# Attention and feed-forward in one kernel: inputs cast to bf16 by the GpSimd DMA queue, feed-forward started one batch earlier

## The chip, the cores and the metric

One core of one Trainium2 chip. The metric is device time of one execution in microseconds (us), the median of three or four runs of a kernel (of seven for the kernel before in the experiments). The span is the time from the first to the last instruction in the profile. Every ratio is taken against runs of the kernel before on the same chip in the same rounds.

## The reference

Eight batches of attention (8 heads, 576 queries, 576 keys plus 16 beacon keys that every query sees, head size 64), then a gated feed-forward over all 4608 tokens:

```python
k_all = np.concatenate([beacon_k, k], axis=2); v_all = np.concatenate([beacon_v, v], axis=2)
scores = scale * np.matmul(q, k_all.transpose(0, 1, 3, 2))      # causal on the last 576 keys
a = softmax(scores); attn = np.matmul(a, v_all)                 # (8, 8, 576, 64)
x = attn.transpose(0, 2, 1, 3).reshape(4608, 512)
g = x @ w_gate                                                  # 512 -> 1536
out = (g * sigmoid(g) * (x @ w_val)) @ w_out                    # float32
```

The inputs are float32; the kernel computes in bf16.

## The kernel before

Work is cut into units that the program weaves together by hand. For a pair of heads: first and second half of the scores (`s_ps`), exponentials on ScalarE, causal selects on POOL (the GpSimd engine), and two PV products (the exponentials times v, one product a head: `pv_ps`, 15 matmuls of 65 columns each). For the feed-forward: a "gv unit" (8 matmuls of 512 columns into `gv_ps`, then tanh on ScalarE and the products `u` and `hT` on VectorE) and single output matmuls into `o_ps`. A batch has four steps, one for each pair of heads. In the views, PE is TensorE, PEld its weight loads, DVE VectorE, ACT ScalarE, SPq the queue of SyncE; `xT` is the attention result x, transposed.

The inputs of batches 2 to 7 travel so: SyncE loads float32 rows into staging tiles; VectorE casts q and k, POOL casts v; SyncE issues DMA transposes that put q and k in the form that the scores need (`qT`, `kT`).

```python
def load_batch(b):                        # 31 DMAs on SyncE
    first = load_kv(nc.sync, "k32", k, beacon_k, b, 0, H)
    load_q(nc.sync, b, 0, H)
    load_kv(nc.sync, "v32", v, beacon_v, b, 0, H)
    return first

def prep_pieces(b):
    pieces = []
    for c in range(NKT):
        pieces.append(
            lambda c=c: (cast_chunk(kb, "k32", c, nc.vector), dma_transpose(kT, kb, 80, b, c)))
        pieces.append(
            lambda c=c: (cast_chunk(qb, "q32", c, nc.vector), dma_transpose(qT, qb, 64, b, c),
                         cast_chunk(vb[b % 2], "v32", c, nc.gpsimd)))
    return pieces
# ... batches 0 and 1: attention alone, q and k transposed by TensorE; then 24 gv units
#     and 36 output matmuls without attention, while batch 2 is loaded; then:
for b in range(2, B):
    for m in range(NPAIR):
        if m == 2 and b + 1 < B:
            pieces = prep_pieces(b + 1)
        G()                               # a gv unit, if one is queued
        scores1(b, m)
        if prev: pv(*prev, 0)
        F(6)                              # six output matmuls, if queued
        # ... two pieces, if m >= 2
        scores2(b, m)
        # ... at m == 1: queue the gv units and output matmuls of earlier batches
        G()
        # ... one piece; second pv; F(6)
        if prev and m == 0:
            x_transpose(b - 1)            # five DMA transposes on SyncE
        if m == 0 and b + 1 < B:
            load_batch(b + 1)
        G()
        # ... two pieces
        prev = (b, m)
```

The softmax here doesn't subtract the row's maximum and nothing guards it: scores larger than these inputs give would overflow.

## Time and profile before

| | before |
|---|---|
| median of 3 runs | 509.77 us (507.91 to 511.09) |
| span of the profiled run | 503.9 us |
| mean granted TensorE clock, as recorded | 0.929 |
| start of batch 3 (its first scores start at 169.9, wait, and go on at 173.4) | 172 us |

The table of stretches, the chain and the waits stand in the prediction below. The queue of SyncE in the timeline, in a batch that loads (start, us held, queue, line, operation, output and input, count):

```profile
227.61 6.42 SPq L257 DMA_TRANSPOSE xT<-x  x5
...
236.01 4.27 SPq L118 DMA_DIRECT2D k<-in_k_dram  x8
...
247.64 4.57 SPq L118 DMA_DIRECT2D v<-in_v_dram  x8
...
253.40 1.25 SPq L166 DMA_TRANSPOSE kT<-kb  x1
```

In this trace the queue issues in program order. After the five x-transposes it issues loads until past 252 us, and only then the first transpose for the next batch. The page's line for the DMA queue that carries these loads (packets, MB, share of 16 engines' span):

```profile
q1 hardware_dynamic: 162400, 47.94, 43.6%
```

### The profile page before, as it was taken

Reading aid. Unit: us, or ns where it says so; the run is one execution under the profiler, and the core shown is the slowest. Engines: PE = TensorE matmul, PEld = TensorE weight load, DVE = VectorE, ACT = ScalarE, POOL = GpSimd, SP = SyncE. Lnnn points to the kernel's source line nnn. Section 1 sums busy time; section 2 is a strip of 40 time slices with the busy share of each in tenths; the row PEclk is TensorE's granted clock in tenths of the full one; section 3 lists DMA queues with packets and bytes.
Section 4 is the critical chain, followed back from the end, with each engine's and each line's share of the span. In section 5 each row is a group of like instructions: output and inputs, shape, how many; then the busy total and the mean of one; then the engine's idle time right before and its main releaser. Section 6 shows DMA issues by size and latency. Waiting matters only on the chain.

```text
span 503.9 us, 7659 instructions
## 1 busy us (share of the span) xinstructions
PE 403.4 (80%) x2718; PEld 192.3 (38%) x2760; DVE 256.1 (51%) x506; ACT 170.7 (34%) x237; POOL 121.5 (24%) x393
## 2 busy tenths in 40 slices
PE   1688879995564259768886997699769998999996
PEld 0355544442232124334332443244324443444442
DVE  2455437885026014735563637454745656456662
ACT  1555413330351134434433443344325441122220
POOL 6554640010135030511141105120503110000000
PEclk9999999999697579879987998899879999999999
DMA  8763896484299329814981397239924102100102
GB/s 166 171 151 89 127 140 111 104 184 104 54 208 181 79 74 204 141 33 97 206 148 44 72 197 186 71 70 194 186 45 69 43 21 69 53 32 21 43 21 104
DMA packets 171078, 54.35 MB, mean 108 GB/s; under 512 B 160592, under 2 KB 166256, under 8 KB 171040
## 3 DMA queue, kind: packets, MB, share of 16 engines
q1 hardware_dynamic: 162400, 47.94, 43.6%
q0 software_dynamic: 6112, 5.33, 6.8%
q10 hardware_dynamic: 2528, 0.61, 0.7%
q8 instruction: 21, 0.34, 0.3%
q14 instruction: 17, 0.14, 0.1%
HBM read 38.27 MB, written 9.44 MB: 95 GB/s over the span
## 4 chain that ended last, share of the span: by engine, by line
PE 52%; SPq 20%; DVE 12%; DMA 8%; issue 3%; ACT 2%; another core or an unknown queue 1%; ACTq 0%; POOL 0%; DVEq 0%; POOLq 0%
PE gv_ps L269 25%; PE o_ps L298 15%; PE pv_ps L228 6%; SPq L257 5%; SPq L118 5%; SPq L106 4%; PE s_ps L191 4%; DVE u L280 3%; DVE hT L283 3%; DMA qT<-qb 3%; DMA v<-in_v_dram 3%; SPq L166 2%; DVE x L237 2%; PE t_ps L158 2%; ACT th L278 1%
## 5 line engine op out<-in xcount | busy, mean ns | idle before, releaser
L200 ACT ACTIVATE p<-s_ps 128x720 bf16<-128x720 f32 (+1 forms) x128 | 105.0, 874 | 126.2 <-PE s_ps L191 118.8
L202 POOL TENSOR_SCALAR_AFFINE_SELECT p<-p 128x112 bf16<-128x112 bf16 (+2 forms) x320 | 82.4, 291 | 201.0 <-ACT p L200 197.4
L278 ACT ACTIVATE th<-gv_ps 128x512 f32<-128x512 f32 x108 | 64.5, 597 | 183.5 <-PE gv_ps L269 160.9
L280 DVE SCALAR_TENSOR_TENSOR u<-th,gv_ps 128x512 f32<-128x512 f32 x108 | 74.1, 686 | 102.0 <-ACT th L278 101.7
L269 PE MATMUL gv_ps<-xT,wg 128*128 128x512 bf16 x419 | 114.9, 393 | 8.2 <-DMA xT<-x 6.6
L298 PE MATMUL o_ps<-wo,hT 128*128 128x512 bf16 x412 | 110.7, 406 | 3.4 <-DVE o_sb L307 2.1
L269 PE MATMUL gv_ps<-xT,wv 128*128 128x512 bf16 x423 | 111.5, 385 | 0.2
L191 PE MATMUL s_ps<-qT,kT 64*128 64x336 bf16 (+5 forms) x384 | 51.0, 343 | 52.6 <-DMA qT<-qb 35.3
L283 DVE SCALAR_TENSOR_TENSOR hT<-gv_ps,u 128x512 bf16<-128x512 f32 x108 | 74.7, 691 | 3.7
L269 PEld LDWEIGHTS <-wg 128*128 128x128 bf16 x432 | 41.6, 100 | 58.2 <-issue 13.6
L269 PEld LDWEIGHTS <-wv 128*128 128x128 bf16 x432 | 43.0, 99 | 53.5 <-issue 4.4
L298 PEld LDWEIGHTS <-hT 128*128 128x128 bf16 x432 | 41.6, 103 | 49.2 <-issue 11.9
L228 PE MATMUL pv_ps<-vb,p 128*128 128x65 bf16 x960 | 49.0, 211 | 10.3 <-DVE x L237 8.1
L228 PEld LDWEIGHTS <-p 128*128 128x128 bf16 x960 | 42.7, 109 | 27.5 <-issue 17.7
L191 PEld LDWEIGHTS <-kT 64*128 64x128 bf16 x384 | 16.3, 105 | 85.5 <-issue 57.9
L307 DVE COPY o_sb<-o_ps 128x512 f32<-128x512 f32 x36 | 24.8, 688 | 37.9 <-PE o_ps L298 36.0
L140 POOL CAST vb<-v 128x512 bf16<-128x512 f32 (+1 forms) x30 | 18.7, 638 | 87.0 <-DMA v<-in_v_dram 87.0
L236 DVE RECIPROCAL rec<-pv_ps 128x5 f32<-128x5 f32 x64 | 12.1, 190 | 42.3 <-PE pv_ps L228 42.3
L237 DVE TENSOR_TENSOR x<-pv_ps,rec 128x320 bf16<-128x320 f32 x64 | 31.5, 492 | 2.2
L140 DVE CAST qb<-q 128x512 bf16<-128x512 f32 (+1 forms) x30 | 13.4, 448 | 29.3 <-DMA v<-in_beacon_v_dram 19.6
L140 DVE CAST kb<-k 128x512 bf16<-128x512 f32 (+1 forms) x30 | 14.1, 470 | 0.0
L158 PE MATMUL t_ps<-ident,kb 128*128 128x128 bf16 (+1 forms) x40 | 5.8, 299 | 8.7 <-DVE kb L135 7.5
(33 smaller groups left out, 69.8 us busy)
## 6 DMA issues: line engine op xcount, KB each, us to landing
out_dram<-o_sb SPq DMA_DIRECT2D x36, 256.0 KB, 2.2
q<-in_q_dram SPq DMA_DIRECT2D x70, 128.0 KB, 3.4
k<-in_k_dram SPq DMA_DIRECT2D x64, 96.0 KB, 2.8
v<-in_v_dram SPq DMA_DIRECT2D x56, 96.0 KB, 3.2
wg<-in_moe_w_gate_dram POOLq DMA_DIRECT2D x4, 384.0 KB, 6.2
wv<-in_moe_w_val_dram POOLq DMA_DIRECT2D x4, 384.0 KB, 7.8
wo<-in_moe_w_out_dram POOLq DMA_DIRECT2D x2, 768.0 KB, 14.0
k<-in_k_dram SPq DMA_DIRECT2D x6, 224.0 KB, 3.3
```

What stands on the lines that cost most here:

```text
L118: eng.dma_start(d[:, 1:4, h, :], src[b, h, 112:496, :].rearrange("(c p) d -> p c d", p=P))
L140: engine.tensor_copy(dst[0:n, c, :, 0:D], stage[name][0:n, c, :, :])
L191: nc.tensor.matmul(s[hh][:, col : col + n], lhsT=kT[b % 2][r, m, P * t : P * t + P], rhs=qT[b % 2][r, m, q0 : q0 + n], start=True, stop=True,)
L200: nc.scalar.activation(p[:, 0:used], s[hh][:, 0:used], ACT.Exp, scale=0.125)
L202: nc.gpsimd.affine_select(out=p[:, col : col + n], in_=p[:, col : col + n], compare_op=ALU.is_ge, fill=0.0, base=base, pattern=[[1, n]], c ...
L228: nc.tensor.matmul(o_ps[:, c, 0 : D + 1], lhsT=pt[2 * (m % 2) + hh][w][:, col : col + P], rhs=vb[b % 2][:, t, h, 0 : D + 1], start=(t == 0 ...
L237: nc.vector.tensor_tensor(out=xs[b][:, :, D * h : D * h + D], in0=o_ps[:, :, 0:D], in1=rec[:].to_broadcast([P, NKT, D]), op=ALU.mult,)
L269: nc.tensor.matmul(ps[:, TOK * half : TOK * half + TOK], lhsT=w[:, kk, P * f : P * f + P], rhs=xT[:, kk, r : r + TOK], start=(kk == 0), st ...
L278: tanh = nc.scalar.activation(th[:], ps[:, 0:TOK], ACT.Tanh, scale=0.5)
L280: nc.vector.scalar_tensor_tensor(out=u[:], in0=th[:], scalar=1.0, in1=ps[:, 0:TOK], op0=ALU.add, op1=ALU.mult)
L283: nc.vector.scalar_tensor_tensor(out=hTs[j][:, f, :], in0=ps[:, TOK:1024], scalar=0.5, in1=u[:], op0=ALU.mult, op1=ALU.mult)
L298: nc.tensor.matmul(st["o"][:], lhsT=hTs[j][:, f, P * i : P * i + P], rhs=wo[:, f, :], start=(f == 0), stop=(f == NF - 1),)
```

## The change

Its intent: take the loads off SyncE and the casts off VectorE and POOL by letting the GpSimd DMA queue cast while it loads, straight into double-buffered bf16 tiles; start the feed-forward while batch 1 still computes its attention, so that the stretch of feed-forward alone disappears. The core of the diff:

```diff
+NPE = 3
     ... (three buffers of o_sb instead of two; in the tail 18 output matmuls ahead instead of 12)
-    stage = {n: static.tile([P, NKT, H, D], FP32, name=n) for n in ("q32", "k32", "v32")}
-    qb = static.tile([P, NKT, H, D], BF16, name="qb")
-    kb = static.tile([P, NKT, H, D], BF16, name="kb")
+    q32 = hT_pool.tile([P, QK], FP32, name="q32", tag="hT")      # batch 0 only
+    q16 = static.tile([P, QK], BF16, name="q16")                 # runs of 1 KB, batches 1 and 2
+    qb = [static.tile([P, QK], BF16, name=f"qb{i}") for i in range(2)]
     ... (k32, k16, kb likewise)
+    def load_runs(b, h0, h1):                                    # 5 DMAs, all on nc.gpsimd
+        load_main(nc.gpsimd, k16, k, b, h0, h1)
+        load_rest(nc.gpsimd, k16, k, beacon_k, b, h0, h1)
+        load_main(nc.gpsimd, q16, q, b, h0, h1)
+        load_rest(nc.gpsimd, q16, q, None, b, h0, h1)
+    def load_tiles(b):                                           # 11 DMAs on nc.gpsimd
+        load_key_tiles(tiles(kb[b % 2]), k, beacon_k, b, 0, H)
+        for c in range(NKT):
+            nc.gpsimd.dma_start(tiles(qb[b % 2])[0:n, c, :, :], q[b, :, P * c : P * c + n, :]...)
     ... (transpose_pair: two VectorE copies from runs to tiles, five TensorE transposes,
          two or three VectorE copies out of PSUM)
     make_identity(nc, ident)
-    load_kv(nc.gpsimd, "v32", v, beacon_v, 0, 4, 8)
+    load_v(0, 0, 4)
+    load_v(0, 4, 8)
+    load_w(0)
     for i in range(2):
-        nc.gpsimd.memset(vb[i][64:P, 4, :, 0:D], 0.0)
+        nc.vector.memset(vb[i][64:P, 4, :, 0:D], 0.0)
     ... (batch 0 alone; then, from batch 1 on:)
+    for s in range(NPAIR, len(steps)):
+        G(); scores1(b, m); pv(*prev, 0); F(6); scores2(b, m)
+        if nxt[0] < NPE:
+            prep_k(*nxt, att, "att")
     ... (m == 1 and b > 1: queue gv units and output matmuls)
+        G(); pv(*prev, 1); F(6)
     ... (m == 0: x_transpose(b - 1))
+        G()
+        if nxt[0] < NPE:
+            prep_q(*nxt, att, "att")
     ... (ten DMA transposes of the next batch from m == 1 on, four a step)
+        if b == 1 and m < 2:
+            load_runs(2, 4 * m, 4 * m + 4)
     ... (b == 1: load_v(2), load_wo)
+        if m == 3 and NPE <= b + 2 < B:
+            load_tiles(b + 2)
+        if m == 1 and NPE <= b + 1 < B:
+            load_v(b + 1, 0, H)
```

## The prediction

> **What bounds the kernel now.** I read the page first, then the chain that ended last, a table of stretches, the waits, and the timeline around the waits. The chain's summary:
>
> ```profile
> PE 52%; SPq 20%; DVE 12%; DMA 8%; issue 3%; ACT 2%; another core or an unknown queue 1%; ACTq 0%; POOL 0%; DVEq 0%; POOLq 0%
> ```
>
> Only half of the end time is TensorE work; a fifth is the SyncE queue issuing DMAs. The stretches (cut at the first scores, the start and end of the first feed-forward, and the starts of batches 2 to 7) show where. Columns: length, busy us of the engines, granted clock, DMA share, GB/s.
>
> ```profile
> 0.00:12.10 12.10, 1.70 (x10) 0.92 (x11) 3.01 (x16) 1.28 (x1) 8.23 (x19) 1.00 0.90 170
> 12.10:69.60 57.50, 43.37 (x446) 27.71 (x447) 28.96 (x82) 26.25 (x32) 34.20 (x104) 1.00 0.67 128
> 69.60:121.00 51.40, 51.05 (x223) 22.65 (x226) 37.45 (x60) 14.33 (x24) 2.89 (x5) 1.00 0.69 134
> 121.00:132.00 11.00, 0.82 (x4) 0.23 (x4) 1.27 (x3) 0.00 (x0) 0.00 (x0) 0.68 0.50 121
> 132.00:172.00 40.00, 21.23 (x182) 9.21 (x185) 11.78 (x26) 13.16 (x16) 13.59 (x45) 0.80 0.74 146
> 172.00:217.60 45.60, 32.35 (x248) 15.26 (x252) 21.25 (x45) 18.36 (x25) 13.42 (x45) 0.84 0.64 125
> 217.60:270.00 52.40, 40.94 (x291) 18.88 (x295) 26.17 (x52) 20.25 (x28) 13.09 (x45) 0.89 0.57 115
> ...
> 372.50:415.00 42.50, 41.76 (x304) 19.48 (x309) 22.17 (x42) 19.73 (x27) 10.03 (x40) 0.94 0.17 39
> 415.00:503.90 88.90, 82.48 (x402) 37.80 (x407) 49.23 (x75) 16.72 (x28) 0.00 (x0) 1.00 0.14 49
> ```
>
> Two stretches are full of TensorE work (the feed-forward at 69.6 and the tail). Batch 7, which loads nothing, takes 42.5 us with TensorE full; batch 4, with loads, 52.4. What the loading batches wait for:
>
> ```profile
> PE s_ps L191 <- DMA qT<-qb: 35.3, 11, 8.1
> ...
> 128.76 0.61 PE L191 MATMUL s_ps<-qT,kT 64*128 64x512 bf16 x2 [7.88 <-DMA qT<-qb]
> ...
> 249.25 0.43 DVE L140 CAST qb<-q 128x512 bf16<-128x512 f32 x1 [5.60 <-DMA q<-in_q_dram]
> ...
> 253.68 0.57 PE L191 MATMUL s_ps<-qT,kT 64*128 64x512 bf16 x3 [2.25 <-DVE hT L283]
> ```
>
> A batch's first scores wait for the last DMA transpose; that waits its turn on SyncE behind 31 loads and 5 other transposes; and VectorE, in order, stands still at a cast whose load has not landed, holding up the hT behind it.
>
> Sizes at full clock, from the chain in order of time (start, us, work):
>
> ```profile
> 36.23 0.95 PE pv_ps L228 x15
> ...
> 42.23 0.77 PE t_ps L158 x5
> ...
> 45.41 0.93 PE s_ps L191 x4
> ...
> 480.99 0.86 PE o_ps L298 x4
> 481.86 1.73 PE gv_ps L269 x8
> ```
>
> The second half of the scores takes 0.76 us there too. So full-clock TensorE work before is 108 gv units x 1.73 = 186.8, 432 output matmuls x 0.215 = 92.9, 32 head pairs x (0.93 + 0.76 + 2 x 0.95) = 115.2, 16 q/k pair transposes x 0.77 = 12.3, 8 x-transposes at about 0.7 = 5.6: 413 us. The span is 503.9, so about 91 us are losses: 10 at the start, 12 in batches 0 and 1, 12 plus a cold clock before batch 2, some 15 in batch 2 and in batch 3, 5 to 9 in each of batches 4 to 6, the rest small.
>
> **What the Trainium skill says.** "TensorE: Matmul & The Clock Gate", Part 1, says an idle window of about 3.4 us halves the matmul clock. The trace agrees: 0.68 in the 11 us with TensorE nearly idle, 1.00 in the full stretches; so lost waits also repay in clock. "DMA: Bandwidth & Descriptors", "SWDGE vs HWDGE vs iDMA", says a cast during DMA goes only through GpSimd, whose cores compute the descriptors. The trace has this for the weights: POOL is held 0.765 us for a wg load of 512 rows, 0.751 for a v load of 384, 0.875 for wo of 768. "Perfetto Trace Analysis", "DMA Instruction — SWDGE (GPSIMD)", says such a recorded interval ends with the descriptors written, not with the data; agreed, as the v loads held POOL 0.75 us and landed 5.0 us after issue.
>
> **The change, part by part.**
>
> Removed: VectorE casts of k and q for batches 2 to 7 (60 x about 0.46 = 27 us of VectorE, little of it on the path in itself), the 46 casts of v on POOL (26 us), and SyncE's 31 load issues per batch (about 0.5 us each). SyncE keeps 10 + 5 transposes at 1.25 us and 4 stores, some 21 us of a batch. In the compiled order the 10 transposes of the next batch come four, four and two at the ends of steps 1, 2 and 3; the last two are free to issue about 6 us into step 3 (after that step's store) and land near 11 us, before the scores that need them at about 13. So the wait for qT should go in batches 3 to 7.
>
> Added on POOL: 11 issues for k and q and 6 for v per batch, up to 1024 rows each. From 0.751 at 384 and 0.875 at 768 I estimate 0.95 us for 1024: 10 us in one block at the end of step 3, and 5.5 at the end of step 1. Selects are about 3 us a step. The block runs from about 8 us of step 3 to 18 or 20; the next step's selects then end at about 23, while PV needs them at about 25. Just hidden.
>
> Added on TensorE: batch 2's q and k transposes (8 x 0.77), minus 4 x 0.7 as batch 1's x goes by DMA: work rises to about 416 us.
>
> Start, which gets worse: in the compiled order VectorE's second instruction, a memset of vb's lower rows, stands after the v loads in the program and waits for two of them, the last being the twelfth DMA on POOL. Twelve issues from 1.6 us at about 0.74 end at 10.4; landing about 13.5 to 14.5. Memsets 0.8, then copy, transpose, PSUM copy for k and again for q: about 4.3 us (the strided PSUM copies I put at 0.65 us, between the 0.466 of the plain bf16 one and the 0.688 of o_sb, plus small ones). First scores at about 19 against 12.1: +7. (The order also zeroes 16 loaded rows of v, which costs no time.)
>
> Batch 0: steps of about 7 to 8 us (6.77 before), the PSUM copies being longer. After steps 0 and 1 POOL issues 11 loads, 8 us, before the next selects, so PV slips by about 1 and then 3 us. Batch 1's first scores at about 50.
>
> Batch 1 with feed-forward: a step has 3 gv units (5.2), scores and PV (3.6) and two transposes (1.54), 10.3 us of work. But the q transposes stand after the third gv unit, and their VectorE copy behind that unit's hT: TensorE waits for tanh 0.60 + u 0.69 + hT 0.69 + copies 0.7 + handovers, about 2.8 us, and about 0.9 more for k and buffers. Step about 14.1; the first, with little gv, about 14.6; batch 1 ends at about 107. Batch 2: 12 + 17 (five x-transposes on SyncE, 6.4 + 2.4 us, delay its first gv unit of chunk 1) + 16 + 11.4; batch 3 starts near 163, with 20 gv units and 30 output matmuls done. Before started it at 172 to 174, with 24 and 84 done. The missing 4 x 1.73 + 54 x 0.215 = 18.5 us put the new kernel about 8 us *behind* at this point.
>
> Batches 3 to end: remaining work 88 x 1.73 + 402 x 0.215 + 5 x 14.3 = 310 us. Losses: 1.5 us in each of five batches (first gv unit waiting for x-transposes that now share the DMA engines with loads), 5 us in the tail, as now. So 163 + 310 + 7.5 + 5 = 486. The 2.8 us stalls plus a 0.77 us transpose come close to the idle window; I add 4 us for cold clock: 490.
>
> From 172 on the kernel before loses 504 - 172 minus its remaining 292 us, about 40; the new one about 12. The gain of 28 there is eaten by half in the first three batches. Timed, 490 x 509.77 / 503.9 = 495.7; I say 494, a little less as my stalls were all taken in full.
>
> **Rivals.**
> 1. *POOL becomes the bound.* If a 1024-row cast DMA holds POOL 2 us rather than 0.95, the block is 22 us, selects come about 9 us late in each of five batches, and the time is about 535. For it: everything is now on one in-order queue, and in the compiled order each POOL DMA also waits for the one eight before it. Against: the flat 0.67 to 0.875 us over 64 to 768 rows.
> 2. *Everything pipelines.* If the copies of batches 1 and 2 run ahead and the stalls shrink, only work is left: 416 + 19 start + 6 batch 0 + 12 = 453 span, about 460. For it: TensorE was at 7.9 of 8 us in batch 7. Against: VectorE is in order, and the copy stands behind hT.
> 3. *The transfers collide.* Loads of 9344 rows of 256 B run when x-transposes do. At 20 ns a packet (0.80 x 16 engines x 8 us for 1.29 MB in the first 8 us) they take 12 us of all engines. If transposes doubled, 3 to 5 us a batch would be lost: about 512.
>
> **Range and chances.** The two halves pull against each other and each is uncertain by some 8 us, more on the slow side: 480 to 511. Faster than 499.6 is likelier than not.
>
> **What would show it.** Right: first scores near 19 us; PE t_ps waits on VectorE of 2 to 3 us in batches 1 and 2; batch 3 at about 163; no qT wait over 2 us after it; batches 4 to 6 at 46 to 48 us; POOL blocks of 10 us. Wrong: POOL issues well over 1 us, PV waiting on selects after batch 2, or batch 3 before 150.

## The result, and the profile after

| | before | after |
|---|---|---|
| median of 4 runs | 508.84 us (506.98 to 511.09) | 455.89 us (454.23 to 457.41) |
| span of the profiled run | 503.9 us | 455.6 us |
| recorded clock | 0.929 | 0.978 |
| start of batch 3 (after: its first gv unit; first scores at 160.7) | 172 us | 158.9 us |
| batches 3 to 7 | 243.0 us | 205.1 us |
| after batch 7 | 88.9 us | 91.6 us |

The ratio is 0.8957, 95% interval 0.8904 to 0.901. Here and below, a ratio is the mean time of one kernel's runs over that of the other's runs of the same rounds, so not quite the ratio of the quoted medians. The changed kernel is 10.4% faster, and its time lies 24 us under the low end of my range.

The summary of the chain that ended last, after:

```profile
PE 62%; DVE 14%; POOL 6%; ACT 5%; another core or an unknown queue 5%; DMA 3%; issue 2%; SPq 2%; POOLq 0%; DVEq 0%
```

SyncE's queue fell from 20% of the end time to 2%; TensorE rose from 52% to 62%. The table of stretches of the kernel after, with the same columns as in the prediction (length, busy us of PE, PEld, DVE, ACT, POOL, clock, DMA share, GB/s); the rows are batch 0's loads, the first step of batch 2, batch 3, and the tail (the clock of 1.00 in the first row stands for no record, see the part on the error):

```profile
0.00:22.90 22.90, 1.45 (x10) 0.92 (x11) 3.76 (x24) 1.28 (x1) 10.57 (x20) 1.00 1.02 165
...
107.90:122.90 15.00, 8.45 (x93) 4.86 (x92) 8.18 (x24) 7.74 (x10) 6.14 (x23) 0.83 0.69 71
...
158.90:199.80 40.90, 39.72 (x305) 18.41 (x309) 23.83 (x44) 20.33 (x28) 22.72 (x57) 1.00 1.03 114
...
364.00:455.60 91.60, 85.23 (x414) 39.07 (x420) 50.52 (x77) 17.32 (x29) 0.00 (x0) 1.00 0.14 47
```

From batch 3 on TensorE is full: 39.7 of 40.9 us, at full clock, while the DMA share is at 1.03 and POOL is busy 22.7 us; none of the two holds it up. Before, the batches that load took 45.6 to 52.4 us. What is lost now is lost early: 22.9 us until the first scores, and steps of batches 1 and 2 that are not full. Their waits (engine, tile, line, releaser, then total us, count, longest):

```profile
DVE vb L373 <- DMA vb<-in_v_dram: 16.4, 1, 16.4
...
PE t_ps L186 <- DVE qb L178: 19.3, 11, 2.5
```

The same in the timeline, where a bracket gives the idle time ahead of an instruction and what ended it; the last two lines are a full step of batch 3:

```profile
17.53 0.27 DVE L373 MEMSET vb<- 64x256 uint32 x1 [16.41 <-DMA vb<-in_v_dram]
...
22.92 1.00 PE L221 MATMUL s_ps<-qT,kT 64*128 64x512 bf16 x4 [0.78 <-DVE qT L189]
...
90.75 0.77 PE L186 MATMUL t_ps<-ident,qb 128*128 128x128 bf16 x5 [2.46 <-DVE qb L178]
...
176.60 0.61 PE L258 MATMUL pv_ps<-vb,p 128*128 128x65 bf16 x15
177.05 1.46 PE L328 MATMUL o_ps<-wo,hT 128*128 128x512 bf16 x5
```

Read starts, not durations, where matmuls are pipelined: the 15 PV matmuls start at 176.60 and the next work at 177.05, so they occupy TensorE for 0.45 us. I had counted 0.95. That line is the key to the error.

The SyncE queue after, in a batch that loads:

```profile
218.66 1.22 SPq L205 DMA_TRANSPOSE kT<-kb  x1
...
238.67 1.21 SPq L205 DMA_TRANSPOSE qT<-qb  x1
```

The transposes now spread over 218 to 240 us, and batch 5's scores come only at 240.9: no wait for qT is left there.

Where the gain arises can be counted. At its start of batch 3 the kernel after is some 13.1 us earlier (172 - 158.9; the two cuts are not the same instruction, see the tables), but has 4 gv units and 54 output matmuls fewer behind it, worth 18.5 us: it is 5 us *behind*, much as predicted. From there to the end it needs 296.7 us against 331.9, with those 18.5 us more to do: it gains 54 us where I had predicted 28.

The kernel after has two faults of data order, which the comparison with the reference lets pass. The memset shown above comes after the v loads and zeroes 16 loaded rows of batch 0's v. And the second half of batch 2's q and k is loaded over heads 6 and 7 of batch 1 before these have been copied out. No run tests why they stay unseen. Put into the numpy reference afterwards, the first changes 16 of the 4608 output rows, by 18% there and 0.2% of the whole (root mean square); the second changes the 576 rows of batch 1, by 1% there: the scores are so small that the softmax is almost uniform. Both are mended in some experiments below, to see whether they cost or save time.

### The profile page after: what moved, and what is told of

Its sections match the earlier page's. It is cut to its first block, busy times and chain, and to the rows that moved or that the text cites. A ratio compares the mean times of both kernels' runs of the same rounds, so it can differ in the third digit from the quotient of the medians.

```text
span 455.6 us, 7472 instructions
## 1 busy us (share of the span) xinstructions
PE 388.6 (85%) x2736; PEld 184.3 (40%) x2780; DVE 245.5 (54%) x506; ACT 170.8 (37%) x237; POOL 193.7 (43%) x477
## 3 DMA queue, kind: packets, MB, share of 16 engines
q0 software_dynamic: 99056, 17.95, 52.2%
## 4 chain that ended last, share of the span: by engine, by line
PE 62%; DVE 14%; POOL 6%; ACT 5%; another core or an unknown queue 5%; DMA 3%; issue 2%; SPq 2%; POOLq 0%; DVEq 0%
PE gv_ps L299 32%; PE o_ps L328 18%; DVE u L310 6%; DVE hT L313 5%; PE pv_ps L258 5%; PE s_ps L221 5%; ACT th L308 5%; POOL vb L146 2%; PE t_ps L186 2%; DMA vb<-in_v_dram 2%; SPq L287 2%; POOL p L232 1%; DMA xT<-x 1%; DVE x L267 1%
## 5 line engine op out<-in xcount | busy, mean ns | idle before, releaser
L232 POOL TENSOR_SCALAR_AFFINE_SELECT p<-p 128x112 bf16<-128x112 bf16 (+2 forms) x320 | 80.3, 297 | 155.8 <-ACT p L230 155.0
L328 PE MATMUL o_ps<-wo,hT 128*128 128x512 bf16 x414 | 103.2, 381 | 3.1 <-DVE o_sb L337 2.1
L328 PEld LDWEIGHTS <-hT 128*128 128x128 bf16 x432 | 39.3, 98 | 42.6 <-issue 3.1
L221 PE MATMUL s_ps<-qT,kT 64*128 64x336 bf16 (+5 forms) x384 | 47.5, 315 | 7.3 <-DVE qT L189 2.4
L258 PEld LDWEIGHTS <-p 128*128 128x128 bf16 x960 | 39.1, 103 | 24.6 <-issue 13.0
L258 PE MATMUL pv_ps<-vb,p 128*128 128x65 bf16 x960 | 45.2, 202 | 4.0 <-POOL p L232 2.4
L146 POOL DMA_DIRECT2D vb<-in_v_dram x44 | 34.4, 809 | 0.1
L186 PE MATMUL t_ps<-ident,qb 128*128 128x128 bf16 (+1 forms) x60 | 8.3, 267 | 19.4 <-DVE qb L178 19.3
L157 POOL DMA_DIRECT2D qb<-in_q_dram x25 | 21.1, 885 | 0.0
L146 POOL DMA_DIRECT2D kb<-in_k_dram x20 | 17.0, 868 | 0.2 <-issue 0.2
```

What stands on the lines that cost most here:

```text
L146: eng.dma_start(dst[0:n, c, h0:h1, 0:D], src[b, h0:h1, r : r + n, :].rearrange("h j d -> j h d"))
L221: nc.tensor.matmul(s[hh][:, col : col + n], lhsT=kT[b % 2][r, m, P * t : P * t + P], rhs=qT[b % 2][r, m, q0 : q0 + n], start=True, stop=True,)
L232: nc.gpsimd.affine_select(out=p[:, col : col + n], in_=p[:, col : col + n], compare_op=ALU.is_ge, fill=0.0, base=base, pattern=[[1, n]], c ...
L258: nc.tensor.matmul(o_ps[:, c, 0 : D + 1], lhsT=pt[2 * (m % 2) + hh][w][:, col : col + P], rhs=vb[b % 2][:, t, h, 0 : D + 1], start=(t == 0 ...
L328: nc.tensor.matmul(st["o"][:], lhsT=hTs[j][:, f, P * i : P * i + P], rhs=wo[:, f, :], start=(f == 0), stop=(f == NF - 1),)
```

## The experiments

Two questions. First: the kernel before had 54 us to win after batch 3 rather than 28; whose were they? Theory S: of SyncE's in-order queue, whose 31 load issues hold back the transposes. Rival V: of VectorE's casts, which stand in order ahead of `hT` and of PSUM copies. Second: did the sizes in my sum fail because of the clock? All kernels here gave results that the comparison accepted.

| run | median us | before | ratio (95%) |
|---|---|---|---|
| m1_memset_first | 445.32 | 506.7 | 0.8777 (0.8735 to 0.8819) |
| m2_q_early | 451.5 | 506.7 | 0.8902 (0.8861 to 0.8943) |
| m3_k16_late | 456.06 | 506.7 | 0.8997 (0.894 to 0.9053) |
| m4_before_swloads | 449.06 | 506.7 | 0.8847 (0.8792 to 0.8903) |
| c1_sp_issues | 502.78 | 508.58 | 0.9893 (0.9826 to 0.996) |
| c3_sp_and_casts | 506.44 | 508.58 | 0.9977 (0.9899 to 1.0054) |
| e1_warm_start | 447.44 | 508.58 | 0.8808 (0.8744 to 0.8871) |
| n2_tiles_from_2 | 434.68 | 508.58 | 0.8572 (0.8501 to 0.8642) |
| n3_free_bank | 425.92 | 508.25 | 0.8368 (0.8316 to 0.8419) |
| n4_spread | 413.93 | 508.25 | 0.8136 (0.8106 to 0.8166) |

### m4_before_swloads: the load part alone, on the kernel before

```diff
 # kernel before, with qb2/kb2: two bf16 tiles each
-            tanh = G()          # and load_batch(2) at f == 5, held back behind it
+            G()                 # load_tiles(2), load_v(2), load_tiles(3) ahead of this loop
-        lambda: (cast_chunk(kb, "k32", c, nc.vector), dma_transpose(kT, kb, ...))
+        lambda: dma_transpose(kT, kb2[b % 2], ...)       # q likewise; no casts
-            if m == 0 and b + 1 < B: load_batch(b + 1)
+            # four pieces at the end of each step from m == 1 on
+            if m == 3 and b + 2 < B: load_tiles(b + 2)   # on nc.gpsimd
+            if m == 1 and b + 1 < B: load_v(b + 1)
```

> The kernel before with only the load part: k, q and v of batches 2 to 7 cast by GpSimd DMA into double bf16 tiles, DMA transposes from step 1 on; batches 0 and 1, and the feed-forward block behind them, as before. Theory A (the gain is the loads: no SyncE backlog, no VectorE casts waiting in order): batches 4 to 7 take 41 us each, none waits for qT over 1 us, batch 2 starts near 122 us, and the time is 425 to 445, so below the changed kernel. Rival B (the gain is the feed-forward woven in from batch 1 on): 475 or more.

Measured: 449.06 us, 57.6 under the kernel before and some 7 *under* the whole change. (By the ratios, 0.8847 against 0.8957, it is 5 to 6 us; the intervals just miss each other.) So the load part carries all of the gain, and the schedule of the first batches, as given, loses some of it again. The edit also issues the transposes one step earlier; it does not tell that apart from the loads' leaving SyncE. The run lies 4 us over my range. What was missing stands in its timeline, at the start of batch 3:

```profile
145.51 0.61 PE L204 MATMUL s_ps<-qT,kT 64*128 64x512 bf16 x2 [5.92 <-DMA qT<-qb]
...
165.96 1.86 PE L282 MATMUL gv_ps<-xT,wg 128*128 128x512 bf16 x4 [6.78 <-DMA xT<-x]
```

Batch 2 is short there, as no feed-forward is woven into it, so batch 3's transposes are issued too late for it.

### c1_sp_issues: SyncE's issues put back into the kernel after, without the data

```diff
+    scr = static.tile([P, 31 * D], FP32, name="scr")
         elif m == 0:
             x_transpose(b - 1)
+            if 2 <= b and b + 1 < B:
+                for i in range(31):      # 16 rows of 256 B each, never used
+                    nc.sync.dma_start(scr[0:16, D*i : D*i+D], k[b+1, 0, 16*i : 16*i+16, :])
```

> The changed kernel with 31 tiny loads a batch (4 KB each, result unused) back on the SyncE queue at the point where the kernel before issues its loads, batches 2 to 6. They cost SyncE about 0.45 us each and the DMA engines almost nothing. Theory S (the loss of the kernel before in its loading batches was SyncE's backlog: transposes behind loads): the qT waits come back, 3 to 6 us a batch, the time rises by 15 to 30 us. Rival V (the loss was VectorE standing in order at casts): under 5 us.

Measured: 502.78 us, so 47 us of the 53 come back; the theory that I favoured is right in kind, but its 15 to 30 us were too few. The timeline of SyncE's queue and of TensorE:

```profile
228.45 14.47 SPq L437 DMA_DIRECT2D scr<-in_k_dram  x31
243.55 1.23 SPq L207 DMA_TRANSPOSE kT<-kb  x1
...
261.65 0.61 PE L223 MATMUL s_ps<-qT,kT 64*128 64x512 bf16 x2 [7.34 <-DMA qT<-qb]
```

31 issues hold the queue 14.47 us, 0.47 each, for 31 x 4 KB. From the first x-transpose to the first transpose for the next batch it is now 22.6 us; in the kernel after it was 8.3. The scores wait 7.34 us, and 3.06 more a few us later: 10.4 us in this batch, against 47 / 5 = 9.4 us for each of five. Over the run TensorE's waits for qT come to 30.5 us. The rest is in part the clock (0.935 recorded, 0.978 without the issues). The stretch of batch 4, here and in the kernel after, separates the two:

```profile
207.80:261.60 53.80, 43.02 (x312) 19.53 (x312) 24.15 (x44) 20.33 (x28) 23.57 (x57) 0.88 0.81 88
...
199.80:240.90 41.10, 40.43 (x308) 18.80 (x313) 24.04 (x45) 20.32 (x28) 23.51 (x58) 1.00 1.06 114
```

Of the 12.7 us lost there, TensorE is idle for 10.1 and busy 2.6 longer. Over the whole span the pages give 34 us more idle time (501.8 - 401.0 against 455.6 - 388.6) and 12 us more busy time for the same matmuls: about three quarters waiting, one quarter slower matmuls (an estimate, as some matmul records are missing).

### c3_sp_and_casts: the casts put back as well

```diff
+    casts(b, m, n): n x nc.vector.tensor_copy(scb, scr[:, c0 : c0 + 512])   # 5 in steps 2 and 3
```

> The same, with 10 casts of 128x512 fp32 a batch back on VectorE where the kernel before had them (steps 2 and 3), each reading a tile that the tiny loads wrote; results unused. Theory S: at most 10 us above the run with the tiny loads alone. Rival V: 20 us or more above it. If both hold, steps 2 and 3 show VectorE idle at the casts waiting for loads, and batches 4 to 6 near the 51 us of the kernel before.

Measured: 506.44 us, 3.7 over c1, with a ratio to the kernel before of 0.9977: the loss is restored. But the intervals of c1 and c3 overlap, so the 3.7 us are not clear of noise. Rival V falls as the main cause: the issues alone were worth 47 us, the casts on top of them a few at most. The casts that stood still on VectorE waited for loads of the same late queue. One limit: VectorE waited only 8.6 us for loads at these casts, against 29.3 us at the casts of the kernel before, as the tiny loads land early; the casts without the issues were not run.

### m1_memset_first: the memsets ahead of the loads

```diff
     make_identity(nc, ident)
-    load_v(0, 0, 4); load_v(0, 4, 8); load_w(0)
     for i in range(2): ... memsets of vb and kT ...
+    load_v(0, 0, 4); load_v(0, 4, 8); load_w(0)
```

> The changed kernel with the memsets of vb, kT ahead of the first v loads, so that VectorE no longer waits for them. Theory (the start is pure loss on the path): first scores move from 22.9 to about 12.5 us and the time falls by 8 to 10 us, to about 447. Rival (batch 0 is paced by POOL's load issues and by v, not by VectorE): first scores move, but batch 0 takes longer, and the time falls by less than 4 us.

Measured: 445.32 us, 10.6 under the kernel after, and one of its two data faults mended.

```profile
9.88 1.00 PE L221 MATMUL s_ps<-qT,kT 64*128 64x512 bf16 x4 [0.78 <-DVE qT L189]
...
34.26 0.58 PE L258 MATMUL pv_ps<-vb,p 128*128 128x65 bf16 x5 [2.06 <-POOL p L232]
```

First scores come at 9.88 instead of 22.92, 13 us earlier; some of it is given back at PV, which now waits for POOL's selects; on POOL these start at 33.89, behind load issues that run from 27.86.

### m2_q_early: q's transposes ahead of the third gv unit

```diff
         if nxt[0] < NPE:
             prep_k(*nxt, att, "att")
+            copy_q(*nxt)                       # the two VectorE copies, early
         G(); pv(*prev, 1); F(6)
+        if nxt[0] < NPE:
+            prep_q(*nxt, att, "att", copies=False)
         G()
-        if nxt[0] < NPE: prep_q(*nxt, att, "att")
```

> The changed kernel with the q copies of batches 1 and 2 right behind those of k, and q's TensorE transposes ahead of the third gv unit. Theory (the 2.34 us waits of t_ps on DVE qb, seven of them, are on the path): PE t_ps <- DVE qb falls from 19 to under 6 us, the time by 9 to 13 us, to about 445. Rival (the wait only moves to the scores or to the psum buffers): the time falls by less than 4 us.

Measured: 451.5 us, only 4.4 under the kernel after, less than half of what I expected (by the ratios some 3, and the intervals overlap, so even that is not clear of noise). The wait named in my prediction fell from 19.3 to 2.6 us, and another stands in its place, 12.1 us in seven waits:

```profile
86.01 0.70 PE L191 MATMUL t_ps<-ident,qb 128*128 128x128 bf16 x5 [2.31 <-DVE x L275]
```

`x` on line 275 is VectorE's multiplication that reads PV's result: the transposes write into the same PSUM bank ("att") as PV, so they wait until PV's result has been read.

### n2_tiles_from_2: batch 2 by tiles and DMA transposes as well

```diff
 # m1, and:
-NPE = 3
+NPE = 2
-        if b == 1 and m < 2: load_runs(2, 4 * m, 4 * m + 4)
-        if b == 1 and m in (1, 2): load_v(2, 4 * m - 4, 4 * m)
+        if b == 1 and m == 0: load_tiles(2)
```

> The changed kernel with the memsets first, and batch 2 fed like batches 3 to 7 (tiles of 256 B rows and DMA transposes instead of 1 KB runs and TensorE transposes); this also gives batch 1 its right q and k. Theory (the transposes of a pair on TensorE with their waits cost about 2.5 to 3 us a step over the 10.3 of a step without them): batch 2 and the preparing steps become 8 to 12 us shorter, to about 435. Rival (the DMA engines, near full there, deliver the rows late): no gain or slower than 445.3.

Measured: 434.68 us. In ratio it goes from m1's 0.8777 to 0.8572, so some 10 us. It also mends the second data fault. One wait of batch 2 is left, for the DMA transposes of x:

```profile
106.87 1.89 PE L299 MATMUL gv_ps<-xT,wg 128*128 128x512 bf16 x4 [7.16 <-DMA xT<-x]
```

### n3_free_bank: the transposes of batch 1 in a bank of their own

```diff
 # n2, and:
-            prep_k(*nxt, att, "att")
+            prep_k(*nxt, outp, "outp"); copy_q(*nxt)
         G()
+        if nxt[0] < NPE: prep_q(*nxt, outp, "outp", copies=False)
         pv(*prev, 1); F(6)
         G()
-        if nxt[0] < NPE: prep_q(*nxt, att, "att")
```

> The 434.7 us kernel (memsets first, batch 2 by tiles and DMA transposes) with batch 1's TensorE transposes of q and k in the psum bank that the output product does not use yet, q's copies behind k's and q's transposes ahead of PV. Theory (what undid the earlier try was the psum bank that the transposes share with PV, not VectorE's speed): the 2.3 to 2.7 us waits of t_ps, four of them, fall below 1 us, the time by 5 to 9 us, to about 428. Rival (VectorE's copies of 1.1 us a pair out of psum are the limit): less than 3 us.

Measured: 425.92 us, 8.8 under n2, as expected. The bank of the output matmuls is unused in batch 1, and with it the move that m2 tried pays. No wait of `t_ps` for `x` is left in the trace. That fits the reading of m2's wait, although bank and order were changed in one edit.

### n4_spread: POOL's issues spread, a gv unit held back for batch 2

```diff
 # n3, and:
         if m < 2: load_runs(1, 4 * m, 4 * m + 4)
-            load_v(1, 4 * m, 4 * m + 4)
         elif m == 2: load_w(1)
-        else: load_w(2); load_w(3)
+        else: load_v(1, 0, H)              # load_w(2), load_w(3) at b == 1, m == 1
-        G()                                # first gv unit of a step
+        if b > 1: G()
```

> The same, with POOL's load issues in batch 0 spread (v of batch 1 after step 3, two weight pieces in batch 1) and one gv unit a step less in batch 1, kept for batch 2. Theory (in batch 0 PV waits 1.5 and 2 us for selects behind load issues, and the first gv unit of chunk 1 waits 7 us for x in batch 2, with no gv unit left to fill it): 6 to 10 us less than the kernel above, to about 420. Rival (the weights or v then come late): no gain.

Measured: 413.93 us (413.24 to 414.31), 12 under n3 where 6 to 10 were expected; 18.6% under the kernel before and about 9% under the kernel after. The busy times of its page:

```profile
PE 382.2 (93%) x2740; PEld 180.8 (44%) x2740; DVE 237.3 (58%) x470; ACT 170.8 (42%) x237; POOL 189.6 (46%) x466
```

TensorE is busy 93% of the span, against 85% in the kernel after. Busy is not full speed, though: part of batch 0 still runs at half clock (last section). The edit spreads the issues and holds back a gv unit at once, and which of the two gained what was not tested.

### m3_k16_late: the second half of batch 2's runs loaded after batch 1 has used them

```diff
-        if b == 1 and m < 2:        load_runs(2, 4 * m, 4 * m + 4)
+        if b == 1 and m in (0, 2):  load_runs(2, 2 * m, 2 * m + 4)
```

> The changed kernel with the second half of batch 2's q and k runs loaded a step later, after heads 6 and 7 of batch 1 have been copied out of the buffer (the given order overwrites them; this run is the correct one). Theory: it costs no time, within 3 us of 456. Rival (POOL is near its limit there, and 5 more issues in that step hold the selects back): 5 us or more slower.

Measured: 456.06 us; the kernel after's 0.8957 lies inside its interval of 0.894 to 0.9053. The second data fault bought no time.

### e1_warm_start: TensorE kept busy with dummy matmuls in batch 0

```diff
 # m1, and:
+    def burst(n): n matmuls, ident x a zero tile of 512 columns, into a PSUM tile never read
+    burst(14)
     prep_k(0, 0, outp, "outp")
+    burst(8)
     # and burst(4) after scores2 and after the second pv of each step of batch 0
```

> The changed kernel with the memsets first (445.3 us) and dummy matmuls of 512 columns on TensorE: 22 before the first scores, 8 a step in batch 0; results unused. Theory (in the kernels so far TensorE runs batch 0 and the whole attention-only stretch at half clock, which the page prints as 1.00 for want of a record): with the clock up, PV of 15 matmuls in batch 0 takes 0.45 to 0.6 us and the 4 first score matmuls about 0.55, as in the later batches, instead of 0.95 and 0.93. Rival (PV there is bound by the rate at which TensorE's instructions are issued when no long matmuls run ahead): PV stays at 0.9 or more. For the time: between 6 us faster and 4 us slower, as POOL and VectorE pace batch 0.

Measured: 447.44 us, no faster than m1, and its sizes are what the run was for:

```profile
21.54 0.62 PE L258 MATMUL pv_ps<-vb,p 128*128 128x65 bf16 x15
22.00 1.03 PE L390 MATMUL d_ps<-dumm,ident 128*128 128x512 bf16 x4
...
39.43 1.01 PE L258 MATMUL pv_ps<-vb,p 128*128 128x65 bf16 x15
40.24 1.49 PE L390 MATMUL d_ps<-dumm,ident 128*128 128x512 bf16 x4
```

PV of a head now takes 22.00 - 21.54 = 0.46 us in batch 0. In the kernel after it took 0.94 there, from start to next start:

```profile
31.82 1.00 PE L258 MATMUL pv_ps<-vb,p 128*128 128x65 bf16 x15
32.76 1.00 PE L221 MATMUL s_ps<-qT,kT 64*128 64x512 bf16 x4
```

This trace has a record of the clock in batch 0, and the column of the clock, last but two, follows it:

```profile
17.30:34.30 17.00, 11.88 (x141) 6.34 (x139) 10.22 (x33) 8.33 (x10) 16.19 (x33) 1.00 1.23 120
34.40:41.10 6.70, 6.22 (x50) 3.42 (x51) 2.49 (x8) 1.43 (x2) 6.70 (x24) 0.50 0.83 90
```

In the second stretch, at half clock, PV goes back to 40.24 - 39.43 = 0.81 us, although dummies run at 37.02 and 40.24, in the same order as before. So it was the clock, and not the rate of issue that the rival named. The time does not fall. That suggests that TensorE's clock does not pace batch 0, but the dummies take TensorE time of their own (400.4 us busy in all, 390.1 in m1), so this run does not show it.

## Why the prediction was wrong

The failed step is the one headed "Sizes at full clock", and with it the sentence "From 172 on the kernel before loses 504 - 172 minus its remaining 292 us, about 40". I took 0.93 for the first scores, 0.76 for the second, 0.95 for a PV and 0.77 for a pair of transposes from the timeline at 36 to 46 us, because the column of the clock says 1.00 there. The trace has no record of the clock before 73.9 us in the kernel before (70.1 in the kernel after); with nothing recorded the column prints 1.00. (So the 1.00 that the prediction read for the full feed-forward stretch covers 4.3 us without a record.) The first record is a rise. The gv matmuls on either side of it show both states, in the timeline of the kernel before; then comes a full step of its batch 7, where the clock is truly up:

```profile
70.90 1.91 PE L269 MATMUL gv_ps<-xT,wv 128*128 128x512 bf16 x4
72.61 1.65 PE L269 MATMUL gv_ps<-xT,wg 128*128 128x512 bf16 x4
74.10 1.03 PE L269 MATMUL gv_ps<-xT,wv 128*128 128x512 bf16 x4
...
379.05 0.61 PE L228 MATMUL pv_ps<-vb,p 128*128 128x65 bf16 x15
379.50 1.46 PE L298 MATMUL o_ps<-wo,hT 128*128 128x512 bf16 x6
...
384.35 1.04 PE L191 MATMUL s_ps<-qT,kT 64*128 64x512 bf16 x4
385.32 0.63 PE L228 MATMUL pv_ps<-vb,p 128*128 128x65 bf16 x15
...
387.18 0.48 PE L191 MATMUL s_ps<-qT,kT 64*128 64x80 bf16 x8
387.60 1.04 PE L269 MATMUL gv_ps<-xT,wg 128*128 128x512 bf16 x4
...
394.63 1.04 PE L191 MATMUL s_ps<-qT,kT 64*128 64x512 bf16 x4
```

Four gv matmuls take 72.61 - 70.90 = 1.71 us, 0.43 each; from 74.10 on four take 0.86, 0.215 each (the next group starts at 74.96). PV takes 0.45 in batch 7. A step with three gv units and twelve output matmuls takes 394.63 - 384.35 = 10.28 us, so a batch 41.1. The prediction's own table contradicted its sum: by the sizes that I used, such a batch needs 12 x 1.73 + 48 x 0.215 + 14.3 = 45.4 us, and the row of batch 7 that I quoted, 42.50 us, is shorter than that. I read that row as "TensorE full" and did not compare.

At the right sizes a pair of heads needs 0.52 + 0.42 + 2 x 0.46 = 1.9 us, not 3.6. The 0.42 is 387.60 - 387.18 above, for the second scores; the 0.52 is what the first scores take in e1 where its clock is recorded as full (17.69 to 18.21). In the full step above they occupy 385.32 - 384.35 = 0.97 us, as the second head's first matmul starts 0.47 us after the first head's; I count those 0.45 us as a gap, not as work. The 20 pairs of batches 3 to 7 therefore hold 34 us less work, and what I took for work in the kernel before was loss: from 172 us on it loses about 332 - (84 x 1.73 + 348 x 0.215 + 20 x 1.9) = 74 us, not 40. The new kernel can win back what is loss, not what is work.

The predicted sum against the measurement, term by term (us of span):

| step | predicted | measured | difference |
|---|---|---|---|
| first scores | 19 | 22.9 | |
| first scores of batch 1 | 50 | 50.1 | |
| end of batch 1 | 107 | 107.9 | |
| start of batch 3 | 163 | 158.9 | -4 |
| batches 3 to 7, each | 45.4 + 1.5 | 41.0 | 5 x -5.9 = -29 |
| added for a cold clock | 4 | none: 1.00 in batch 3 and in the tail | -4 |
| after batch 7 | 83.3 + 5 | 91.6 | +3 |
| whole span | 490 | 455.6 | -34 |

Of the 5.9 us a batch, 4 x (3.6 - 1.9) = 6.8 is the wrong size and 1.5 the x-transpose waits that did not come; against it stand some 2.4 us of small gaps between matmuls which I had not counted, 4 x 0.45 of them in the first scores. The 4 us at the start of batch 3 come from the middle two steps of batch 2, 24.1 us for 33 predicted; its first step took 15.0 for 12.

What was right:
- The waits for qT and for the casts are gone, and SyncE's queue is off the chain. That the queue was the lever is shown by c1, but I had stressed VectorE standing still at a cast as much as the queue. The queue alone was worth 47 us.
- POOL's issues cost what I worked out: 0.885 us in the mean for q's tiles (0.95 estimated for 1024 rows, 0.90 to 0.94 measured), and the block at the end of a batch hides beside other work. Rival 1 falls. Rival 3 falls too: the DMA share in batch 3 is 1.03 and TensorE is full beside it.
- The late start comes from the memset that waits for v loads. It is 4 us later than I said, yet batch 1 begins on time, by luck, as batch 0 took 27.2 us rather than 31. m1 shows that the memset is worth 10.6 us.
- In batches 1 and 2 TensorE waits for VectorE's copies of q, up to 2.5 us a step (2.8 predicted), and batch 1's steps take 13.5 to 15.9 us (14.1 predicted; that this fits is partly luck, as the sizes in it were the wrong ones and the clock there is full only in part). But this wait has another behind it, the bank shared with PV, as the trace of m2 shows and n3 bears out; what I thought worth its full length was worth 4.4 us at most alone.
- The first three batches do put the new kernel behind in work done: by 5 us (8 predicted).

Rival 2, "everything pipelines", named 460 us and came within 5, but for other reasons: it also used 416 us of work and let the stalls of batches 1 and 2 vanish, which they did not.

What stays open: what the casts would cost without SyncE's issues, and what the second head's first score matmul waits for.

## What to carry to other kernels

Take an instruction's full-clock size only from a stretch whose clock is proven by a known neighbour (here four matmuls of 512 columns in 0.86 us), and hold the sum of the sizes against a stretch that is known to be full before using it. An in-order queue that issues DMAs counts as busy nowhere, yet small issues in front of a transpose that the next batch needs can cost more than all casts (47 us here, against some 4): count issues, not bytes, and put loads and dependent transposes on different queues. When a wait is removed, look for the next resource behind it, such as a shared PSUM bank, and move both at once.

## What the Trainium skill lacked or had wrong

- "DMA: Bandwidth & Descriptors", "Issuing engines are not separate DMA queues", says that starting DMAs from several engines only saves the sequencer's issue time, "which is usually small relative to the DMA itself". For a single DMA the trace agrees: a k load of the kernel before took 4.27 / 8 = 0.53 us to issue and 2.8 us in the median to land. What the passage leaves out is the sum: 31 issues of 4 KB on SyncE, 0.47 us each, ahead of transposes on the same queue, made the kernel 47 us slower (c1).
- "TensorE: Matmul & The Clock Gate", Part 1, says when idleness halves the clock, and Part 4 that transposes do not count as busy in the same way. (No run here separates transposes from other matmuls.) Neither says how dense a mix of small matmuls and transposes has to be to raise it. In the fastest kernel (n4) such a stretch stayed at half clock: PV takes 26.45 - 25.51 = 0.94 us in it, and the clock's first record is a rise at 47.2 us. Yet TensorE's busy time was 27.85 of 35 us, at that clock. The table prints 1.00 for it, for want of a record:

```profile
25.51 1.00 PE L266 MATMUL pv_ps<-vb,p 128*128 128x65 bf16 x15
26.45 1.00 PE L229 MATMUL s_ps<-qT,kT 64*128 64x512 bf16 x4
...
10.00:45.00 35.00, 27.85 (x258) 16.72 (x254) 21.05 (x65) 16.38 (x20) 31.51 (x77) 1.00 1.23 138
```

- No page that I found says that a profile's clock is unknown, not full, before its first record. (That the array starts throttled does stand in the same Part 1, and agrees with the half speed before that record; I should have asked why the column said otherwise.) In the kernel before that was the first 73.9 us, with 512-column matmuls at 0.43 us, and it misled the prediction by about 30 us.
- "DMA: Bandwidth & Descriptors", "Anatomy of one DMA", calls the time to generate descriptors "small, variable" and gives no number. POOL's recorded interval for one issue was 0.751 us for 384 rows (not cast), 0.875 for 768 and 0.90 to 0.94 for q's tiles of 1024 (both cast).
- No page that I found gives the price of casting in the DMA. The line below, of the kernel after, makes 0.522 x 16 x 455.6 / 99056 = 38 ns of an engine for a packet, as a mean of the whole queue; the line of the kernel before shown above makes 0.436 x 16 x 503.9 / 162400 = 22 ns. The two queues do not carry the same mix of transfers, and apart from v's loads at the start (16.4 us on VectorE, 2.7 on POOL) no wait for this queue's data stands among the longest of the kernel after.

```profile
q0 software_dynamic: 99056, 17.95, 52.2%
```
